# K and V loads of a two-layer decode step: one transfer of 128 partitions, or two of 64

## The chip, the cores and the metric

The kernel runs on one core of a Trainium2 chip. The metric is device time in microseconds (us) of one execution. TensorE (PE) multiplies matrices, VectorE (DVE), ScalarE (ACT) and GpSimd (POOL) work on rows, SyncE (SP) issues transfers, and 16 transfer (DMA) engines move data from the chip's main memory into the 128 partitions of the on-chip memory.

## The reference: what is computed

Two layers of one decode step for four sequences (batch `b`), each an attention block with a cache and a gated feed-forward block, both layers with the same weights and caches:

```python
def _A_ref(x, k_cache, v_cache, wq, wo):      # x: 4 x 1 x 512
    q = (x @ wq) ...                          # 32 heads of 128
    k = jnp.repeat(k_cache, 4, axis=1)        # 4 x 8 x 4096 x 128, bf16
    v = jnp.repeat(v_cache, 4, axis=1)
    scores = jnp.einsum("bhqd,bhkd->bhqk", q, k) * (128 ** -0.5)
    o = jnp.einsum("bhqk,bhkd->bhqd", softmax(scores), v)
    return o... @ wo
def _B_ref(x, w_gate, w_up, w_down):          # 512 -> 1792 -> 512
    h = sigmoid(x @ w_gate) * (x @ w_up)
    return h @ w_down
x = x + _A_ref(layernorm(x), ...)
x = x + _B_ref(layernorm(x), ...)
# and the same two lines once more: the second layer
```

For each of the 32 pairs of sequence and key head (a "unit") K and V are 4096 x 128 numbers of bf16, 1 MB each.

## The kernel before

**Units and buffers.** The work is a sequence of 64 units: 32 for each layer, in an order written out by hand (`ORDER`, L125). Units are taken in pairs. A K or V of a unit fills one slot: 128 partitions of 8 KB, where partition p holds 32 neighbouring rows of the cache, which are 8 KB in one piece in memory. There are 12 slots (`NSLOT`, L114); late in the kernel the four parts of the buffer of `wq` become four more (`yield_wq`, L978). The table `KEPT` (L124) says which K and V of layer 0 stay in their slots until layer 1; the others are loaded again.

**What a unit does.** VectorE transposes K in its slot (`k_turn`, L984 to L993). TensorE multiplies it with q (`scores`, L1009), and once these matrix products are issued, the slot of K is put back on the list `free` unless it is kept (L1021). Then come the maximum, the exponential on ScalarE (L1063), transposes of the probabilities (L1081, L1133) and the products with V (`pv`, L1179), after which V's slot goes back (L1192). The order of these steps over all pairs is a string of letters, `PROGRAM` (L133), that `step` carries out letter by letter; the feed-forward block and the next projection of one sequence at a time are fitted in between.

**Loads.** The order of loads is a string of letters too, `LOADS` (L129): `k` and `v` for a unit's K and V, `o`, `g`, `u`, `d` for parts of the weights. After each step `pump` (L343) issues loads in that order, as long as `free` has a slot. Every load goes out on SP's queue: weights at L349, K and V at L369, `wq` at L382 ahead of all. The very last V is loaded as two halves of columns, each over all 128 partitions, with semaphores of their own (L363 to L365). In program order SP executes nothing but these issues and their waits.

**Waits.** `S.dma` (L82) puts a transfer on an engine's list. Its semaphore, one for each slot (`d0`, `d1`, ...), goes up by 16 when the transfer has landed. `writes=[key]` makes the transfer wait for the last writer and all readers of the slot, and makes the transfer the new last writer (L62 to L74). Who reads the slot later waits for the semaphore value of the last writer. `emit` (L95) turns these into wait instructions (L106) ahead of the waiting instruction.

Of the kernel before, what the change touches and what calls it, by code (L numbers as in the profile page):

```python
# [111 lines left out]


NSLOT = 12  # L114

# [28 lines left out]
def bass_interleave_layers__gqa_block_cached__glu_gated_glu__decode_kernel(  # L146
# [17 lines left out]
    P = 128  # L164
# [19 lines left out]
    S = _Sched()  # L184
# [4 lines left out]
    def sbt(shape, dtype, name):  # L189
        cnt[0] += 1  # L190
        return es.enter_context(nc.sbuf_tensor(f"{name}_{cnt[0]}", list(shape), dtype))
# [3 lines left out]

    slot = [sbt([P, NJ * DH], dt.bfloat16, f"slot{i}") for i in range(NSLOT)]
    wq_sb = sbt([P, KD, HQ * DH], dt.bfloat16, "wq")
# [20 lines left out]
    def small(*shape, dtype=dt.float32):  # L218
# [63 lines left out]
        list(ENGINES)  # L282
        + [f"d{i}" for i in range(NSLOT + KD)]
        + [f"wq{i}" for i in range(KD)]
# [51 lines left out]

    free = list(range(NSLOT))
    where = {}

    def take():  # L340
        return free.pop(0)

    def pump():  # L343
        while loads:
            kind, n = loads[-1]
            if kind in wparts:
                loads.pop()
                dst, src = wparts[kind](n)
                S.dma("sp", (lambda dst, src: lambda e: e.dma_start(dst, src))(dst, src), f"wo{n}" if kind == "wo" else kind, writes=[f"{kind}{n}"])  # L349
                continue  # L350
            if not free:
                return
            loads.pop()
            s = take()
            _, b, u = seq[n]
            if kind == "k":
                where["kn", n] = s
                src = A_k_cache[b, u].rearrange("(p j) d -> p (j d)", p=P)
            else:
                where["v", b, u] = s  # L360
                src = A_v_cache[b, u].rearrange("(p j) d -> p (j d)", p=P)
            parts = [(slot[s][:, :], src, f"d{s}", f"s{s}")]
            if kind == "v" and n == NU - 1:  # L363
                h = NJ * DH // 2
                parts = [(slot[s][:, 0:h], src[:, 0:h], "vh", "vh"), (slot[s][:, h:], src[:, h:], f"d{s}", f"s{s}")]  # L365
            for dst, frm, sem, key in parts:
                deps = S.readers.get(f"s{s}", []) + [S.last_write.get(f"s{s}")] if key == "vh" else ()
                S.dma(
                    "sp", (lambda dst, frm: lambda e: e.dma_start(dst, frm))(dst, frm), sem, writes=[key], deps=deps  # L369
                )  # L370

    def dve(fn, reads=(), writes=()):
        return S.inst("dve", fn, reads=reads, writes=writes)
# [5 lines left out]
    for n in range(KD // 2):  # L379
# [4 lines left out]
            writes=[f"wq{2 * n}", f"wq{2 * n + 1}"],  # L384
        )
    pump()

    S.inst("pool", lambda e: e.memset(qz_sb[:, :, :, :, :], 0.0), writes=QZ + ["pf"])
# [6 lines left out]
        writes=["pe0"],  # L395
    )
    dve(lambda e: e.transpose(pidx[:, :], iota_f[:, 0:32]), writes=["pe0"])
    for a in range(4):
# [6 lines left out]
            writes=[f"ident{a}"],  # L405
# [5 lines left out]
    for k in range(KD):  # L411
# [13 lines left out]
        writes=[f"x{b}" for b in range(Bn)],  # L425
# [552 lines left out]
    def yield_wq():  # L978
        for k in range(KD):
            S.last_write[f"s{NSLOT + k}"] = S.last_write[f"wq{k}"]  # L980
            S.readers[f"s{NSLOT + k}"] = list(S.readers[f"wq{k}"])
            free.append(NSLOT + k)

# [454 lines left out]
    head_masks()  # L1438
    k_turn(0)
    pump()  # L1440
    k_turn(1)
    pump()
    q_mm(Bn, 0, HQ)
    q_spread(0, Bn)
# [100 lines left out]
    for c in PROGRAM:  # L1545
# [29 lines left out]
        writes=["sel_row"],  # L1575
# [4 lines left out]
        writes=["rowk"],  # L1580
# [3 lines left out]
    for part in range(2):  # L1584
# [21 lines left out]
        writes=["o_row"],  # L1606
# [56 lines left out]
```

## Time and profile before

| | |
|---|---|
| median of 3 runs | 307.3 us (307.11 to 307.53) |
| the profiled execution, its own time | 307.37 us |
| its span in the profile | 305.6 us |
| busy: PE, DVE, ACT, POOL | 73%, 63%, 39%, 13% of the span |
| mean granted TensorE clock | 0.699 |
| read from main memory | 116.66 MB, 382 GB/s over the span |
| DMA packets | 20,361 |

How to read it: "span" is from the first to the last instruction of the profiled execution; times inside the trace count from the span's start. A "packet" is one piece that one transfer engine moves. A row of slices divides the span into 40 equal parts; a digit is the busy share in tenths, 9 for 90% or more. In the chain of waits, a line is a start, a duration and the work that ended last at that time; a DMA in it stands for the time from the issue of a transfer to its landing. In the lists of waits, the columns are the total wait, the number of waits and the longest one. "SPq" is SP's own sequence of instructions.

### The profile page before, as it was taken

To read this page: it belongs to the slowest core of one execution; us is meant where nothing else is said; L and a number is where in the kernel's file an instruction comes from. 1 tells how busy PE (TensorE), PEld (TensorE's weight loads), DVE (VectorE), ACT (ScalarE), POOL (GpSimd) and SP (SyncE) were. 2 spreads that over 40 slices of the span, in tenths; PEclk is the share of its full clock that TensorE was granted. 3 is DMA by queue.
4 is the path that set the end of the run, shared out by engine and by line. 5 is a ranking of instruction groups with operands and counts; after the bars stand their busy time and mean duration, and the time that the engine had idled before them with its cause. 6 is when DMAs were issued, how large, how long until landed. Compare 5 with 4: busy or idle time off the path is not lost.

```text
span 305.6 us, 11315 instructions
## 1 busy us (share of the span) xinstructions
PE 222.4 (73%) x4872; PEld 150.2 (49%) x4872; DVE 193.8 (63%) x414; ACT 118.1 (39%) x413; POOL 40.3 (13%) x205
## 2 busy tenths in 40 slices
PE   1223565147769699999899689885789799887886
PEld 1221243124636366647456556543556574564575
DVE  6344966254513587598946486757696777678443
ACT  1001152223503257731546625334466423557600
POOL 0002111001100212111113010112021010321000
PEclk9999999999995555557756556595555576657555
DMA  7999999999999999999999999999999999999930
GB/s 292 417 426 406 409 408 381 388 419 410 415 406 409 365 388 375 425 420 417 417 417 415 416 324 416 419 402 415 420 421 418 389 368 371 365 421 423 415 132 3
DMA packets 20361, 117.38 MB, mean 384 GB/s; under 512 B 1876, under 2 KB 5976, under 8 KB 7640
## 3 DMA queue, kind: packets, MB, share of 16 engines
q1 hardware_dynamic: 20288, 116.66, 95.0%
q8 instruction: 38, 0.62, 0.8%
q14 instruction: 11, 0.09, 0.1%
q10 hardware_dynamic: 24, 0.01, 0.0%
HBM read 116.66 MB, written 0.00 MB: 382 GB/s over the span
## 4 chain that ended last, share of the span: by engine, by line
DMA 50%; PE 29%; DVE 10%; issue 4%; SPq 3%; ACT 2%; POOL 1%; DVEq 0%; POOLq 0%; ACTq 0%
DMA slot<-in_A_v_cache_dram 18%; DMA slot<-in_A_k_cache_dram 15%; DMA wq<-in_A_v_cache_dram 11%; PE S_ps L1009 8%; DVE slot L993 8%; PE O_ps L1179 7%; DMA wd<-in_B_w_down_dram 6%; PE M_ps L885 3%; SPq L369 2%; PE M_ps L839 2%; PE M_ps L934 2%; DVE small L1026 1%; PE M_ps L814 1%; ACT pT L1133 1%; PE PT L1081 1%
## 5 line engine op out<-in xcount | busy, mean ns | idle before, releaser
L993 DVE STREAM_TRANSPOSE slot<-slot 128x1024 f32<-128x1024 f32 (+2 forms) x70 | 105.0, 1507 | 18.6 <-DMA slot<-in_A_k_cache_dram 15.3
L1133 ACT ACTIVATE pT<-PT 32x128 bf16<-32x128 f32 x236 | 63.1, 268 | 57.8 <-PE PT L1081 27.8
L1009 PE MATMUL S_ps<-slot,qz 128*16 128x256 bf16 x992 | 62.1, 398 | 18.3 <-DVE slot L993 8.1
L1179 PE MATMUL O_ps<-pT,slot 128*128 128x4 bf16 x1792 | 57.0, 166 | 21.2 <-DMA slot<-in_A_v_cache_dram 13.5
L1179 PEld LDWEIGHTS O_ps<-pT,slot 128*128 128x128 bf16 x1792 | 52.9, 103 | 34.9 <-DMA slot<-in_A_v_cache_dram 17.7
L1063 ACT ACTIVATE wide<-S_ps,small 128x256 bf16<-128x256 f32 x64 | 30.3, 473 | 44.6 <-DVE small L1056 18.9
L1009 PEld LDWEIGHTS S_ps<-slot,qz 128*16 128x16 bf16 x992 | 27.8, 113 | 39.1 <-DVE slot L993 10.7
L709 POOL COPY qz<-qs 32x32 bf16<-32x32 bf16 x128 | 26.0, 203 | 110.6 <-ACT qs L694 52.8
L1026 DVE TENSOR_REDUCE small<-S_ps 128x2 bf16<-128x512 f32 x32 | 21.7, 678 | 17.3 <-PE S_ps L1009 15.4
L1081 PE MATMUL PT<-ident_bf,wide 128*128 128x64 bf16 (+1 forms) x288 | 18.7, 227 | 3.4 <-ACT wide L1063 3.3
L1081 PEld LDWEIGHTS PT<-ident_bf,wide 128*128 128x128 bf16 x288 | 15.2, 122 | 10.0 <-ACT wide L1063 8.1
L1210 DVE TENSOR_TENSOR oT<-O_ps,small 128x8 bf16<-128x8 f32 (+1 forms) x32 | 5.3, 166 | 22.3 <-PE O_ps L1179 21.5
L1092 POOL CAST small<-small 128x2 bf16<-128x2 f32 x32 | 5.9, 184 | 99.0 <-ACT wide L1063 82.1
L1049 DVE SCALAR_TENSOR_TENSOR O_ps<-O_ps,small,wide 128x128 f32<-128x128 f32 x32 | 11.2, 349 | 8.7 <-PE O_ps L1035 6.8
L885 PE MATMUL M_ps<-wq,small 128*1 128x512 bf16 x128 | 14.6, 598 | 0.0
L1236 PE MATMUL AC<-wo,oT 128*1 128x512 bf16 x96 | 11.4, 576 | 2.1 <-DMA wo<-in_A_wo_dram 1.9
L1063 ACT ACTIVATION_READ_ACCUMULATOR wide<-S_ps,small 128x1 f32 x64 | 12.3, 193 | 0.0
L694 ACT ACTIVATE qs<-M_ps 128x128 bf16<-128x128 f32 x8 | 1.9, 280 | 25.0 <-PE M_ps L683 24.9
L1035 PE MATMUL O_ps<-ident_bf,small 128*128 128x64 bf16 x64 | 8.6, 225 | 4.1 <-DVE small L1026 1.8
L1056 DVE TENSOR_REDUCE small<-O_ps 128x2 f32<-128x128 f32 x32 | 9.3, 292 | 3.2 <-ACT wide L1063 0.5
L900 ACT ACTIVATE t_row<-M_ps,small 128x512 bf16<-128x512 f32 x4 | 2.7, 687 | 21.4 <-PE M_ps L885 18.7
L1147 PEld LDWEIGHTS O_ps<-small 128*128 128x128 bf16 x124 | 6.1, 107 | 7.7 <-POOL qz L709 1.7
(142 smaller groups left out, 209.4 us busy)
## 6 DMA issues: line engine op xcount, KB each, us to landing
slot<-in_A_v_cache_dram SPq DMA_DIRECT2D x48, 1024.0 KB, 9.8
slot<-in_A_k_cache_dram SPq DMA_DIRECT2D x44, 1024.0 KB, 11.4
wq<-in_A_wq_dram SPq DMA_DIRECT2D x2, 2048.0 KB, 10.0
wo<-in_A_wo_dram SPq DMA_DIRECT2D x8, 512.0 KB, 17.6
wq<-in_A_v_cache_dram SPq DMA_DIRECT2D x3, 1024.0 KB, 10.2
wq<-in_A_k_cache_dram SPq DMA_DIRECT2D x2, 1024.0 KB, 13.0
wu<-in_B_w_up_dram SPq DMA_DIRECT2D x2, 896.0 KB, 10.6
wg<-in_B_w_gate_dram SPq DMA_DIRECT2D x2, 896.0 KB, 10.6
```

Source lines behind the costliest of these rows:

```text
L709: (lambda a, ps: lambda e: e.tensor_copy(qz_sb[ps, :, :, a, :], qs_sb[b][ps, :, u * REP:(u + 2) * REP].rearrange("p t (u r) -> p u t r", r ...
L885: (lambda k, st: lambda e: e.matmul(M_ps[h][32 * st:32 * st + 1, :], lhsT=xc_bf[:, k, 0:1], rhs=wv[:, k, h, :, st, :], start=(k == 0), sto ...
L993: dve(lambda e: e.transpose(kf, kf), writes=[f"s{st}"])
L1009: (lambda t, b2, e_, c, x1, r0: lambda e: e.matmul(S_ps[p][r0:r0 + 4 * REP, half], lhsT=qz_sb[:, part, t, :, :].rearrange("p a r -> p (a r)"),
L1026: dve(lambda e: e.tensor_reduce(rm_bf, S_ps[p].rearrange("p (u n) -> p u n", u=2), AX.X, ALU.max), reads=[f"S{p}"], writes=["rmb"])
L1049: lambda e: e.scalar_tensor_tensor(out=shifted, in0=maxima, scalar=rowk_f, in1=mask_f.rearrange("p n w -> p (n w)").unsqueeze(1).broadcast ...
L1056: dve(lambda e: e.tensor_reduce(nm_sb, shifted, AX.X, ALU.min), reads=[f"O{n}"], writes=["nm"])
L1063: (lambda u, half: lambda e: e.activation(pe_sb[:, half], S_ps[p][:, half], ACTF.Exp, bias=nm_sb[:, u:u + 1], scale=exp_scale, accum_out=s ...
L1081: (lambda w, a0, a1, c0: lambda e: e.matmul(PT[:, c0:c0 + 16 * (a1 - a0)], lhsT=wide_sb[:, NV + 64 * w:NV + 64 * w + P], rhs=valid_bf[:, : ...
L1133: (lambda dst, frm: lambda e: e.activation(dst, frm, ACTF.Copy))(dst, frm),
L1179: (lambda n, x, c, j: lambda e: e.matmul(bank[:, ul * REP:(ul + 1) * REP], lhsT=vv[:, x * JG + c * 4 + j, :], rhs=pT[:, x % 2, ul, j, 2 * ...
L1236: (lambda r, h, i: lambda e: e.matmul(AC[32 * r:32 * r + 1, :], lhsT=oT_sb[:, h, own_column:own_column + 1], rhs=wo_sb[:, h, :], start=(j ...
```

## The change

Each K or V load of 1 MB becomes two transfers: one of partitions 0 to 63 and one of partitions 64 to 127, each of 64 rows of 8 KB. Both stand one behind the other on SP's queue and add 16 to the same semaphore. The first takes over the waits for the slot; the second has none of its own, and becomes the slot's last writer, so that readers wait for the sum of both. Weights stay in one transfer, and so do the two column halves of the last V.

```diff
 NSLOT = 12
+PIECES = 2
...
             for dst, frm, sem, key in parts:
                 deps = S.readers.get(f"s{s}", []) + [S.last_write.get(f"s{s}")] if key == "vh" else ()
-                S.dma(
-                    "sp", (lambda dst, frm: lambda e: e.dma_start(dst, frm))(dst, frm), sem, writes=[key], deps=deps
-                )
+                n = 1 if kind == "v" and len(parts) > 1 else PIECES
+                for h in range(n):
+                    rows = slice(P // n * h, P // n * (h + 1))
+                    issue = (lambda dst, frm: lambda e: e.dma_start(dst, frm))(dst[rows, :], frm[rows, :])
+                    if h == 0:
+                        S.dma("sp", issue, sem, writes=[key], deps=deps)
+                    else:
+                        S.last_write[key] = S.dma("sp", issue, sem)
```

## The prediction

> **What bounds the kernel now.** I read the page's slices and queue lines first, then the chain of waits in order of time, then SP's own waits, then the DMA packets one by one.
>
> ```profile
> span 305.6 us, 11315 instructions
> ...
> DMA  7999999999999999999999999999999999999930
> GB/s 292 417 426 406 409 408 381 388 419 410 415 406 409 365 388 375 425 420 417 417 417 415 416 324 416 419 402 415 420 421 418 389 368 371 365 421 423 415 132 3
> ...
> q1 hardware_dynamic: 20288, 116.66, 95.0%
> ```
>
> From the second slice to the 38th the transfer engines are busy in nine tenths or more of the time, and one queue (q1, SP's) moves all 116.66 MB. No compute engine is near that (PE 73% of the span, DVE 63%).
>
> ```profile
> 121.70 11.13 DMA slot<-in_A_v_cache_dram
> ...
> 142.31 10.40 DMA slot<-in_A_v_cache_dram
> ...
> 160.76 10.73 DMA slot<-in_A_v_cache_dram
> ...
> 258.56 10.16 DMA wq<-in_A_v_cache_dram
> ...
> 269.85 23.74 DMA wq<-in_A_v_cache_dram
> 293.63 0.59 PE S_ps L1179 x16
> ```
>
> The chain that ends last runs through loads; between them stand a few us of compute that give a buffer back. The first half of the last load lands at 293.6 us, its second half 1.2 us later, and the work on the last unit follows.
>
> ```profile
> SPq L106 <- PE O_ps L1179: 93.1, 36, 11.0
> SPq L106 <- PE S_ps L1009: 47.1, 16, 5.6
> ...
> L369 SPq DMA_DIRECT2D slot<-in_A_v_cache_dram x48: 327/328/5861, 1.6 to 266.8; - x48
> ...
> DMA to landing us min/median/max: 5.4/10.4/27.7
> ```
>
> SP, which issues every load, waits 140 us in all for PE to give a slot back (L106), and one issue takes it 0.33 us in the median. A load lands 10.4 us after its issue, though one lands every 2.48 us in the full stretches: some four are queued.
>
> The packets say what a load costs. A 1 MB load is 128 packets of 8 KB, eight for each of 16 transfer engines; of the 12,416 such packets the fastest took 307 ns and the median one 309. Packets of 4 KB took 159 ns and of 1 KB 46 ns, so time goes with bytes plus about 8 ns. A semaphore packet (4 bytes, one for each engine at the end of a load) took 9 ns. 8 x 309 + 9 = 2481 ns, which is the pace of the landings: every engine runs at its floor. Counted for one engine, all data packets and semaphores come to 278 us, while the stream lasts from 1.7 to 294.8 us; ten landings that come 2.9 to 4.3 us after the one before, instead of 2.5, hold some 10.5 us of the difference.
>
> **The change part by part.** Section 6 of the page counts what is split:
>
> ```profile
> slot<-in_A_v_cache_dram SPq DMA_DIRECT2D x48, 1024.0 KB, 9.8
> slot<-in_A_k_cache_dram SPq DMA_DIRECT2D x44, 1024.0 KB, 11.4
> ...
> wq<-in_A_v_cache_dram SPq DMA_DIRECT2D x3, 1024.0 KB, 10.2
> wq<-in_A_k_cache_dram SPq DMA_DIRECT2D x2, 1024.0 KB, 13.0
> ```
>
> That is 48 + 44 + 3 + 2 = 97 loads; the last V stays in two column halves of 128 partitions, and weights stay whole.
>
> 1. *Issues.* 97 more at 0.33 to 0.5 us are 32 to 49 us of SP's time. They lie in its 140 us of waiting, and the second piece goes out while at least the first piece's 1.24 us (4 x 309 ns) are queued. I count 0; if that cover were gone, each would show 0.33 us. At the start, where SP is already held in single issues for 5 to 10 us because so much is outstanding, the loads stand behind 4 MB of wq anyway.
>
> 2. *Waits.* The deps stand on the first piece, the readers' wait on the second's semaphore value, which both pieces must reach. No consumer starts earlier, none waits for more bytes. 0.
>
> 3. *Semaphore packets.* Each engine gets one more per load: 97 x 9 ns = 0.87 us, on the path while the queue is full.
>
> 4. *Bytes and packets.* The same 8 KB rows, 128 for a load: 0 from packet count.
>
> 5. *Where the packets land.* This is the open price. Before, a load covers all 128 partitions, and each engine writes 8 of them. After, if 64 rows still spread over all 16 engines (four rows each, as I assume), all write into 64 partitions first, then all into the other 64. The trace has no load of large rows into fewer than 128 partitions (x, four rows of 1 KB, is too small to tell), so it can't say whose floor the 309 ns are. Lower bound: the engines' own; the packets stay at 309 ns. Upper bound: the way into the partitions; half of them then take half the bytes, a packet takes 618 ns, and a load 8 x 618 + 18 = 4962 ns, 2.48 us more: 97 x 2.48 = 241 us.
>
> [...]
>
> I take a value between the bounds, nearer the upper. If two engines share a way, they halve each other only while both are in the same half; one that is ahead by d gets the other half's way for itself for that long. A half then costs 2 x 1.236 - d us of data instead of 1.236. For d: the 16 engines of the first loads finish 0.80 us apart, or 0.05 us from one to the next, since they are started one after another; if the two that share are eight apart in that order, d = 0.4. A load takes 2 x (2.47 - 0.4 + 0.009) = 4.16 us, 1.68 more than 2.48, and 97 x 1.68 = +163 us. Later the 16 engines land 1.7 to 3.8 us apart, so that d wanders; with d even between 0 and 1.24 a load would take 1.5 x 2.48 = 3.72 us (+120). But a load is complete when its slowest pair is, and a pair that runs ahead drains the queue and starts again beside its partner. So I keep d = 0.4.
>
> 6. *What is late next.* With loads at 4.16 us compute has slack, and of the 10.5 us in which the queue ran short I take half as gone: -5. The 11 us after the last landing stay.
>
> Sum against the profiled execution: 307.4 (305.6 of span and 1.8 around it) + 163 + 0.9 (inside the 163 already) - 5 = **465 us**. The median of the runs is 307.3, so the two agree.
>
> **The rivals.**
>
> *Lockstep (0.18).* The partners keep no lead, d near 0, as after any moment when all restart together. 307.4 + 241 = 548 us. For it: ten stalls at which all engines stop and restart. Against it: 38 instruction fetches of 16 KB (about 1 us each on one engine) push single engines out of step.
>
> *No sharing, and slower by the semaphores (0.12).* The floor is the engines' own: 307.4 + 0.9 = 308.3. For it: time per byte is the same for 1, 4 and 8 KB packets, as a limit inside the engine would make it. Against it: a limit at the place written would look alike, since each engine here has its own 8 partitions. If the two pieces go to eight engines each, this case holds too.
>
> *No sharing, within 0.2% (0.11).* The same, but at least 0.3 of the 0.87 us falls where the queue is short and slots are waited for: 307.4 to 308.0.
>
> *Not slower but faster (0.07).* Place: the ten stalls. There the engines start anew one after another, 0.05 us each with eight rows to describe; with four rows the last could start up to 0.4 us sooner. Price: up to 10 x 0.4 = 4 us less, against the 0.87 more: 304.3 to 308.3. It decides from 0.15 us of gain in each stall (10 x 0.15 - 0.87 = 0.6 us), and only if packets into 64 partitions stay at 309 ns.
>
> That the change does not do what it says can hardly be: the issue counts would show 97 loads instead of 194.
>
> **How the numbers follow.** Forecast (partners share a way, with a lead between them): 0.52, own range 410 (d wandering freely, 307 + 120 less the stalls, is 417) to 510 (d = 0.2, 307 + 202). The rest as above. About 0.2% (0.6 us) is what a measurement of this kernel can tell from no change. Slower: 0.52 + 0.18 + 0.12 = 0.82; same 0.11; faster 0.07. Forecast's own range, lockstep and no sharing all have to be reached to leave out no more than 2 in 10: 306.8 (only the faster case stays out below) to 552 (lockstep with its bound).
>
> **What would show it.** Step 5: packets of 8 KB at around 618 ns in large part and 309 in the rest (only 309 would refute it; only 618 would be lockstep); landings every 4.2 us; the GB/s slices near 250 where they are near 415; the DMA busy digits still 9. Steps 1 and 2: SP's issue count 194 for these loads, its waits for PE much shorter. Step 6: fewer stalls, PE and DVE shares of the span down by a third, the granted clock up from 0.70. It is wrong altogether if packets keep 309 ns; then the price of the change is the semaphores'.

## The result and the profile after

The changed kernel takes 515.06 us (median of 4 runs, 511.26 to 517.27) against 307.21: 1.678 times the time before, with an interval of 1.664 to 1.692. The profiled execution took 517.27 us, its span is 515.4.

The page of the changed kernel, its span, its slices and its queue:

```profile
span 515.4 us, 11412 instructions
...
DMA  8999999999999999999999999999999999999970
GB/s 341 222 231 226 232 229 217 219 251 269 339 214 223 223 223 226 230 224 231 234 228 223 225 223 226 223 224 230 228 237 238 235 233 230 228 228 230 230 180 8
...
q1 hardware_dynamic: 21840, 116.67, 97.2%
```

The transfer engines are as busy as before and move the same bytes, but the slices stand near 225 GB/s where they stood near 410. Only where weights go in one piece of 128 partitions does the rate come up (slice 1 with 341, slices 10 and 11 with 269 and 339). The chain of waits in order of time shows the same pattern as before with longer loads:

```profile
188.85 18.59 DMA slot<-in_A_v_cache_dram
...
210.27 20.15 DMA slot<-in_A_v_cache_dram
...
232.60 20.59 DMA slot<-in_A_v_cache_dram
```

The tile view of the slots has SP's issues (count, then shortest, median and longest in ns) and the time to landing:

```profile
L372 SPq DMA_DIRECT2D slot<-in_A_v_cache_dram x96: 465/596/10553, 1.7 to 455.9; - x96
L372 SPq DMA_DIRECT2D slot<-in_A_k_cache_dram x88: 465/597/7134, 2.9 to 448.9; - x88
...
DMA to landing us min/median/max: 6.4/18.3/42.9
```

Twice the issues, each longer (0.60 us for 0.33), and a landing 18.3 us after its issue instead of 10.4. SP's waits for PE did not shrink, they grew from 140 to 236 us:

```profile
SPq L106 <- PE O_ps L1185: 146.8, 33, 16.9
SPq L106 <- PE S_ps L1015: 88.8, 17, 12.4
```

The packets of 8 KB carry the difference. They are as many as before (12,416), but their median is 587 ns where it was 309, and their mean 575 where it was 322; only 52 of them took less than 320 ns. A semaphore packet took 17.5 ns in the mean, before 9.4. Eight packets and two semaphores make 8 x 575 + 2 x 17.5 = 4.64 us a load. By means a load before was 8 x 322 + 9 = 2.59 us, and 97 x 2.05 = 199 us of the 208 are explained so. The rest is packets of other sizes, which became slower too. The queue's share closes the sum: packets of q1 held each engine for 95.0% of 305.6 us, which is 290, and now for 97.2% of 515.4, which is 501. That is 211 us more, while the time without a packet is 15 us before and 14 after.

### The profile page after: what moved, and what is told of

Read it like the earlier page. It is cut to its first block, busy times and chain, and to the rows that moved or that the text cites. A ratio compares the mean times of both kernels' runs of the same rounds, so it can differ in the third digit from the quotient of the medians.

```text
span 515.4 us, 11412 instructions
## 1 busy us (share of the span) xinstructions
PE 229.7 (45%) x4872; PEld 150.2 (29%) x4872; DVE 195.4 (38%) x414; ACT 118.2 (23%) x413; POOL 40.3 (8%) x205
## 3 DMA queue, kind: packets, MB, share of 16 engines
q1 hardware_dynamic: 21840, 116.67, 97.2%
## 4 chain that ended last, share of the span: by engine, by line
DMA 68%; SPq 14%; PE 7%; issue 4%; DVE 3%; ACT 2%; POOL 1%; DVEq 0%; POOLq 0%
DMA slot<-in_A_v_cache_dram 32%; DMA slot<-in_A_k_cache_dram 29%; SPq L372 12%; DMA wq<-in_A_v_cache_dram 8%; PE S_ps L1015 3%; DVE slot L999 2%; PE O_ps L1185 2%; SPq L350 2%; ACT wide L1069 1%; ACT pT L1139 1%; POOL qz L715 1%; PE PT L1087 0%; PE S_ps L1595 0%; PE M_ps L491 0%; PE O_ps L1335 0%
## 5 line engine op out<-in xcount | busy, mean ns | idle before, releaser
L1015 PE MATMUL S_ps<-slot,qz 128*16 128x256 bf16 x992 | 62.5, 401 | 49.5 <-DVE slot L999 29.1
L1015 PEld LDWEIGHTS S_ps<-slot,qz 128*16 128x16 bf16 x992 | 26.4, 112 | 73.7 <-DVE slot L999 30.3
L906 ACT ACTIVATE t_row<-M_ps,small 128x512 bf16<-128x512 f32 x4 | 2.7, 687 | 41.8 <-PE M_ps L891 34.1
L1041 PEld LDWEIGHTS O_ps<-ident_bf,small 128*128 128x128 bf16 x64 | 4.2, 108 | 19.1 <-DVE small L1032 11.5
## 6 DMA issues: line engine op xcount, KB each, us to landing
wq<-in_A_wq_dram SPq DMA_DIRECT2D x2, 2048.0 KB, 10.5
```

The costliest lines, as they stand in the source:

```text
L1015: (lambda t, b2, e_, c, x1, r0: lambda e: e.matmul(S_ps[p][r0:r0 + 4 * REP, half], lhsT=qz_sb[:, part, t, :, :].rearrange("p a r -> p (a r)"),
L1041: (lambda u: lambda e: e.matmul(O_ps[n][:, P + 64 * u:P + 64 * u + 64], lhsT=rm_bf[:, u:u + 1].broadcast_to([P, P]), rhs=valid_bf, start=T ...
```

## The experiments

The theory, S: all 16 engines write into one half of the partitions at a time, and a half takes only half the rate. Rivals: N, the number or the size of the transfers costs the time wherever they land; M, the memory read does (512 KB in one piece, four rows an engine).

**Loads by themselves, m1_stages.** SP issues stages of loads and waits after each; nothing is computed. The list of a stage, here for halves in turn and for partitions 32 to 95:

```python
[("buf", 64 * h, 64 * h + 64, W * i, W * i + W, i) for i in range(8) for h in range(2)]
[("buf", 32, 96, W * i, W * i + W, i // 2) for i in range(16)]
```

> This kernel computes nothing of the reference: it only loads, in eight stages of 8 MB each, each stage waiting for the one before, and its time stands for itself. Pieces are 64 partitions x 8 KB unless said otherwise. Theory S (sharing at the place written: all 16 engines in one half of the partitions get half the rate): a stage at full rate is 8 x 2.48 = 20 us plus some 2 us of start and landing, one at half rate 40 plus 2. Theory N (many or small transfers cost the time, wherever they land). Theory M (the memory read is to blame: 512 KB in one piece, four rows an engine). Stage 1, whole loads of 128 partitions: all 22 us. Stage 2, halves in turn as in the changed kernel: all 36 to 42. Stage 3, the lower half only: S 42, N and M 42. Stage 4, partitions 32 to 95 only (half of them from each half of the partitions): S 22, N and M 36 to 42. Stage 5, two column halves of 128 partitions: S and M 23, N 36 to 42. Stage 6, halves in turn in pieces of 4 KB columns: S with the lead of the prediction (0.4 us) 30, S without any lead 42. Stage 7, halves in turn behind a load of 8 rows, which lies on eight engines and puts them 1.24 us behind: if those share with the other eight, S 24; else 37 to 43. Stage 8, the same with two such loads (2.5 us, a whole turn): 38 to 45.

The windows of the eight stages, from the first packet to the last landing (start and end, length, no compute, clock, DMA share, GB/s):

```profile
1.80:23.00 21.20, 0.00 (x0) 1.00 0.96 395
24.40:64.10 39.70, 0.00 (x0) 1.00 0.98 211
65.30:107.10 41.80, 0.00 (x0) 1.00 0.98 201
108.40:130.80 22.40, 0.00 (x0) 1.00 0.92 375
131.80:154.40 22.60, 0.00 (x0) 1.00 0.97 370
155.70:192.30 36.60, 0.00 (x0) 1.00 0.98 229
193.30:233.70 40.40, 0.00 (x0) 1.00 0.97 208
234.60:276.00 41.40, 0.00 (x0) 1.00 0.97 205
```

Halves in turn take 39.7 us, hardly less than the lower half alone (41.8). Partitions 32 to 95 are also 64 rows of 8 KB in 512 KB pieces, and take 22.4; two column halves take 22.6. So it is neither the number, nor the size, nor the memory read: N and M fall, and what counts is in which partitions the rows of a piece lie. Stage 6 measures the lead of the prediction: pieces of 4 KB should have taken 30 us with a lead of 0.4 us and took 36.6. A gain at each change of half is there, but small: against the 41.8 us of stage 3, stage 2 gained 2.1 us in 15 changes and stage 6 gained 5.2 in 31, which is 0.14 and 0.17 us a change. Stage 7 tells nothing: the load ahead was over at 193.9 us, before the first half's packets began at 194.1. In stage 8 the loads ahead ended at 235.7 us, when the halves had begun at 235.6; eight engines then stayed 0.5 us behind the other eight to the end, without any gain.

**Two column halves, e1_cols.**

```diff
-                    rows = slice(P // n * h, P // n * (h + 1))
-                    issue = ...(dst[rows, :], frm[rows, :])
+                    part = slice(NJ * DH // 2 * h, NJ * DH // 2 * (h + 1)) if n > 1 else slice(None)
+                    issue = ...(dst[:, part], frm[:, part])
```

> Each K or V load is two transfers as in the changed kernel, but of 128 partitions and half of the columns. S (sharing at the place written): 16 packets of 4 KB at 159 ns and two semaphores make 2.56 us a load instead of 2.48, so 307 + 97 x 0.08 = 315 us. N (many or small transfers): some 515 us. M (the memory read): between, since each engine now reads 4 KB pieces 8 KB apart; 315 if pieces of memory do not matter.

315.58 us, 1.032 (1.025 to 1.040) times the time before: S to within a us, priced from the rows of 4 KB packets. As many transfers and bytes as the change, and 9 us instead of 208.

**Even and odd partitions, e5_even_odd.**

```diff
-                    rows = slice(P // n * h, P // n * (h + 1))
+                    rows = bass.ds(h, P // n, step=n)
```

> The changed kernel with one edit: the two transfers of a load take the even and the odd partitions. As many transfers, rows, bytes, issues and semaphores as the change, but each covers both halves of the partitions. S (the rate is shared within a half of the partitions): no price but the semaphores' 97 x 9 ns, 307 + 0.9 = 308 us; every price of the change lies in where its pieces land. If pieces of 64 rows, their issues or their memory read carry part of the price, more: each us above 308 is theirs. If the last engine of each load starts sooner after a stall because only four rows are described, below 307, by 4 us at most.

308.82 us, 1.0057 (1.0026 to 1.0088). The page of this kernel:

```profile
span 307.0 us, 11412 instructions
...
GB/s 299 415 423 410 409 408 379 391 417 402 414 410 370 370 381 369 424 416 401 419 363 394 423 367 400 423 399 406 416 422 421 415 391 381 393 423 423 412 95 3
```

The same instructions as the change (11,412), the same 64-row transfers, and the full rate: its 8 KB packets are at 309 ns in the median. All the price of the change but 1.7 us is in which partitions a piece holds. Of the 1.7 us, 0.9 were expected for semaphores; the rest (the interval reaches from 0.8 to 2.7) isn't told apart.

**Four pieces of 32 partitions, e4_four** (`PIECES = 4`).

> PIECES is 4: each K or V load is four transfers of 32 partitions. If the rate went with the number of partitions that a transfer covers, a load would take 4 x 2.48 = 9.9 us and the kernel 307 + 97 x 7.4 = 1030 us. If 32 partitions reach as much as 64 (sharing by halves of the partitions), about 515 as with two pieces, and 194 more semaphores make 2 us at most of difference. If the number of transfers cost the time, 307 + 3 x 208 = 930 us.

Two runs, 497.7 and 509.8 us: not slower than two pieces. The price goes neither with the number of transfers nor with the partitions that one covers; 32 partitions of a half do as well as its 64.

**Middle, bottom and top, e2_mid.**

```diff
-                for h in range(n):
-                    rows = slice(P // n * h, P // n * (h + 1))
+                pieces = [slice(0, P)] if n == 1 else [slice(32, 96), slice(0, 32), slice(96, 128)]
+                for h, rows in enumerate(pieces):
```

> Each K or V load is three transfers: partitions 32 to 95, then 0 to 31, then 96 to 127. S: half of the bytes go at full rate and two quarters at half rate, 1.24 + 2.48 = 3.72 us a load at most, 307 + 97 x 1.24 = 427 us; by the measured price of the change (208 of 241 us) 411. So faster than the changed kernel although there are more transfers. N: more than 515 us, by the number of transfers some 610. M: not below 515.

477.73 us: faster than the change with one transfer more, as only S has it, but 51 to 67 us above what S priced. **One kind alone** missed in the same way. e3_k_only cuts K and e6_v_only cuts V (`n = PIECES if kind == "k" else 1`, and the like):

> Only the 46 loads of K are cut into halves, V stays whole. All theories in which each cut load pays for itself: 307 + 46/97 x 208 = 406 us. If one half load beside whole loads finds the other half free, less: the whole loads ahead and behind let engines drift apart, and the price is below 99 us.

> Only the 51 loads of V that the change cuts are cut into halves; K stays whole. K alone cost 148 us (455 against 307), where 46 loads at 2.15 us would make 99. If a mixed stream always costs more than its share, V alone costs some 51 x 3.2 = 163 us, 470; if each cut load pays 2.15 us, 307 + 110 = 417; if K's loads are dearer because VectorE and the scores wait for them first, V alone is below 417.

K alone: 455 us in the faster of two runs (the other 474). V alone: 472.66. That is (455.3 - 306.8) / 46 = 3.2 and (472.7 - 307.2) / 51 = 3.2 us for each cut load, against 208 / 97 = 2.1 where all are cut. A stream that is mixed costs more than its share. A small part of that is idle transfer engines: q1's packets fill 93.9% of the 472.0 us span of e3_k_only (the slower run) and 92.6% of the 468.7 of e6_v_only, which leaves 29 and 35 us without a packet, against 14 in the change. The next two kernels ask for the rest, and why the lead is worth so little.

**More stages, m2_stages.** A load of 8 rows of 32 KB goes ahead in stage 3, two in stage 4; stages 5 to 8 cut loads in other ways.

> Computes nothing of the reference: eight stages of 8 MB of loads, one after the other; its time stands for itself. The earlier stages showed that partitions 32 to 95 alone load at full rate, so sharing at the place written holds; open is why two engines never get out of each other's way. L (lead kept): two engines that share stay as far apart as they start. A (pulled into step): a lead is lost within a few packets. Stage 1, whole loads: 22 us. Stage 2, halves in turn: 39 as before. Stage 3, halves behind a load of 8 rows of 32 KB, which lies on eight engines and takes 2.1 us, some 0.8 us of it before the halves start, so that these eight are 1.3 us behind, one half's full-rate work: L, if they share with the other eight, 24 to 27; A 39 to 41. Stage 4, two such loads, 3.4 us behind: L 30 to 40, A 41 to 43. [...] Stage 6, partitions 32 to 95, then 0 to 31, then 96 to 127: 32 by full, half and half rate, 36 by the price measured in the kernel. Stage 7, whole load and halves in turn: 31 if each half load pays 2.3 us for itself, 35 if the whole loads pay too, as the kernel with K alone in halves suggests. Stage 8, quarters of 32 partitions: 39 if 32 partitions reach as much as 64, 78 if the rate goes with the number of partitions.

```profile
1.80:23.00 21.20, 0.00 (x0) 1.00 0.95 394
24.60:63.90 39.30, 0.00 (x0) 1.00 0.98 213
64.80:108.90 44.10, 0.00 (x0) 1.00 0.95 196
109.80:158.70 48.90, 0.00 (x0) 1.00 0.93 182
160.00:182.70 22.70, 0.00 (x0) 1.00 0.92 369
184.10:214.80 30.70, 0.00 (x0) 1.00 0.97 273
215.90:246.50 30.60, 0.00 (x0) 1.00 0.95 273
247.50:286.70 39.20, 0.00 (x0) 1.00 0.99 213
```

Stage 3: the eight packets ahead took 2.9 to 4.0 us, where I had priced 2.1, so eight engines began with the halves 1.3 to 3.0 us after the others. While they ran, the other eight, which wrote into the same half (56 of its 64 rows lie outside partitions 0 to 7), fell from 0.31 to 0.39 us a packet to 0.94 to 1.29. From 70.6 us on, 6 us into the stage, all 16 engines began their packets within 0.2 us of one another. But these were not packets of the same transfer. The semaphores of each half came in two groups of eight (69.85 to 70.08 us and 71.31 to 72.02 for the first half, 106.07 to 106.19 and 107.25 to 107.97 for the last), so that eight engines stayed 1.1 to 2.2 us behind the other eight to the end. For much of each turn of 2.4 us eight engines were in one half and eight in the other, and their packets took some 0.6 us all the same. After 106.2 us the late eight were alone, all in the upper half, and their last packets still took 0.51 to 0.65 us.

So the stage decides neither for L nor for A: a distance between these eights is kept, and it gains nothing. A half's rate is then not simply divided among all the engines that write there at the time, as S has it. The engines that share may lie within the same eight; the trace does not name the engine of a packet, and this stays open. Stage 5 is the even and odd form at the full rate (22.7 us). Stages 6 and 7 take 30.7 and 30.6 us, about what S prices (32 and 31); the kernel's surplus for mixed streams isn't in them.

**Pushed out of step, m3_stages.** Stages of 20 loads; stages 3 to 5 have a small load of eight packets of 8 KB after every fourth load, as a push.

> Computes nothing of the reference: five stages of 20 MB of loads; its time stands for itself. Question: why K alone in halves costs 3.2 us a cut load in the kernel, while whole loads and halves in turn cost 2.15 us a cut load in the stage of 8 MB. Whole 2.48 us, cut 4.63. Stage 1, whole and cut in turn: 10 x 7.11 + 2 = 73 if nothing but length differs; 83 if a longer stream falls out of step. Stage 2, in an order like the kernel's first loads with K cut (11 of 20): 9 x 2.48 + 11 x 4.63 + 2 = 75; 86 at the kernel's price. Stage 3, as stage 1 with a load of 8 rows, which lies on eight engines, after every fourth load (5 in all, 0.6 us each): 73 + 3 = 76 if the engines fall back into step, 86 if a push out of step is what costs. Stage 4, all cut, with the same pushes: 95 + 3 = 98, more if pushes cost. Stage 5, all whole, with the same pushes: 52 + 3 = 55.

```profile
1.80:77.40 75.60, 0.00 (x0) 1.00 0.99 277
78.40:156.60 78.20, 0.00 (x0) 1.00 0.99 268
157.60:255.40 97.80, 0.00 (x0) 1.00 0.97 218
256.60:358.20 101.60, 0.00 (x0) 1.00 0.99 210
359.20:416.00 56.80, 0.00 (x0) 1.00 0.98 375
```

A mixed stream without pushes costs about what it should (75.6 and 78.2 us, where 73 and 75 were expected), and five pushes make it 22 us longer; they make the whole loads some 4 us longer (56.8 against 20 x 2.65 = 53 by stage 1 of the other kernels) and the cut loads some 3 (101.6 against 20 x 4.91 = 98). So a push cost the mixed stream some 4.4 us (22 / 5), and the others under one (4 / 5 and 3 / 5). That the engines fall out of step there is my reading, and was not measured by itself. What the packets show: of the 2,600 packets of 8 KB in stage 3 there are 524 that took over 750 ns, of the 2,560 in stage 1 only 6. In the kernels with K or V alone, too, there are 521 and 357 of 12,416, against 114 in the change, and the 16 increments of a transfer's semaphore come 5.0 and 4.9 us apart in the median, in the change 3.0, before 2.1. That the 38 instruction fetches of 16 KB, each on one engine (1.02 us each in the mean before, 1.27 in the change), do the pushing there fits, but was not tried by itself; nor was e2_mid's surplus.

## Why the prediction was right or wrong

The direction and the cause were right: where the pieces land sets the price. The size was short by 50 us (465 for 515). The range held the time, but the forecast's own range (410 to 510) just missed it: the outcome lies between the forecast and lockstep (548), nearer to lockstep.

- *Steps 1, 2 and 4 (issues, waits, packets)* held: e5_even_odd has all of them and costs 1.7 us. An issue takes 0.60 us, not 0.33 to 0.5, and is still hidden. That SP would wait much less for PE was wrong: 236 us instead of 140.
- *Step 3 (semaphores)*: 9 ns held at full rate (9.2 in e5_even_odd); in the shared half they take 17.5 ns, of no weight.
- *Step 5 (where the packets land)* is where it failed. Sharing was right: packets went from 309 to 575 ns, near the upper bound of 618. The term that was mis-sized is the lead d = 0.4 us, and with it 4.16 us a load: measured 4.64. In the step's own formula that is a lead of 0.17 us, 2 x (2.47 - 0.17 + 0.0175), and stages 2 and 6 of m1_stages have 0.14 and 0.17. With 4.64 in place of 4.16 the step's price is 209 us, and the forecast would have been 511. Why the gain is so small isn't shown: in stage 3 of m2_stages two groups of eight stayed 1.1 to 2.2 us apart and gained nothing, so a lead between those groups is not what pays. That the two that share are eight apart, from which d = 0.4 came, was my assumption, and no run shows it; the trace names no engine of a packet. That the value lay nearer the upper bound was a choice, too, for which no run stood yet. By stages 2 and 3 of m1_stages halves in turn gain 5% over one half alone (39.7 against 41.8 us).
- *Step 6 (the next limit)*: packets of weights and of the last V became slower too, which the prediction left out: 1 KB packets from 49.5 to 80.1 ns in the mean, 256 for each engine, are 7.8 us, the other shapes some 4. That half of the stalls goes isn't shown. The 10.5 us before were hardly time without packets (of those 15 us, 12.5 lie ahead of the stream and behind it) but long packets: the mean of 322 ns over the median of 309 makes 776 x 12.7 ns = 9.9 us for each engine. In the change such packets are inside the mean of 575, and what became of them can't be told apart.
- *Lockstep* came nearer to the time, with too dear a packet (618 for 575). *No sharing* in its three forms is refuted by the packets and by e5_even_odd, which shows what it would have been: 308.8, so slower by the semaphores, and no gain after stalls.
- *What would show it*: packets near 618 or 309 in two groups did not come, 92% lie in one group between 480 and 650. GB/s near 225, not 250. PE's share fell from 73 to 45%, by a little more than the third that was said. The granted clock did not rise from 0.70 in the profiled run; it was 0.66.

## What to carry to other kernels

When loads are cut along the partitions, cut so that each piece covers both halves of them: columns and even and odd rows cost little or nothing here (e1_cols 315.6 us, e5_even_odd 308.8, against 307), while the lower and the upper 64 in turn took nearly the double time per byte (39.7 us for 8 MB, whole loads 21.2, m1_stages). The middle 64 loaded at the full rate (22.4 us), but the quarters that they leave over did not: e2_mid took 478 us. A median packet time at nearly twice its floor (587 ns for 307), with the engines busy (q1's packets held them for 97.2% of the span), was the mark of it. The trace of before showed a floor of 307 ns and not whose it was, the place written or the engine, so before sizing such a change load something by itself into part of the partitions.

## What the runs showed of the hardware that was not expected

- Partitions 32 to 95 loaded at the full rate (22.4 us for 8 MB, whole loads 21.2) and so did the even and the odd ones (22.7), but the lower 64 took 41.8 and quarters of 32 in turn 39.2. Which rows each engine takes of such a piece the trace doesn't show.
- Eight packets of 32 KB into partitions 0 to 7, the second load ahead in stage 4 of m2_stages, took 4.83 us each and side by side: 262 KB in 4.83 us, 54.3 GB/s for eight partitions. The first load ahead, which began on idle engines, was through in 4.27 us (61 GB/s); why it was faster stays open.
- While eight packets of 32 KB went into partitions 0 to 7, the packets of the other eight engines into the lower half went from 0.31 to 0.39 us to 0.94 to 1.29 (stage 3 of m2_stages). After that the 16 engines began packets within 0.2 us of one another, though eight of them were 1.1 to 2.2 us behind in the work.
- Eight engines alone in the upper half still took 0.51 to 0.65 us a packet (the end of stage 3 of m2_stages), as when all 16 were there.
- Whole and cut loads in turn lost 22 us to five small pushes: 97.8 against 75.6 us for the same 20 MB, nearly the 101.6 us of a stage in which every load was cut.
